# The opening of a fused attention and gated-unit kernel: another way to turn batch 0's q, more filler products, a split copy and an earlier sigmoid table

## Chip, cores and metric

One NeuronCore of one Trainium2 chip. The metric is the time of one execution in device microseconds. The engines are named as in the profile: PE is TensorE (its weight loads are PEld), DVE is VectorE, ACT is ScalarE, POOL is GpSimd, SP is the queue that issues most DMAs.

## What is computed

A linear attention without softmax for 8 batches, 8 heads, 576 tokens and a head size of 64, with a root-mean-square norm per head, followed by a gated linear unit whose gate comes from a causal convolution of 5 taps. All is fp32; the weights of the second block arrive as 64-bit floats.

```python
def _attn_ref(q, k, v, g_norm):
    kv = np.einsum('bhsd,bhse->bhde', k, v)
    out = np.einsum('bhsd,bhde->bhse', q, kv)
    rms = np.sqrt(np.mean(out * out, axis=-1, keepdims=True) + 1e-06)
    return (out / rms * g_norm).astype(np.float32)

# x: out with the heads side by side, (8, 576, 512)
def _moe_ref(x, w_val, conv_w, w_out):
    xp = np.concatenate([np.zeros((B, K - 1, D)), x], axis=1)
    for k in range(K):
        gate_pre += conv_w[k][None, None, :] * xp[:, k:k + S, :]
    gate = 1.0 / (1.0 + np.exp(-gate_pre))
    val = x @ w_val
    return (gate * val @ w_out).astype(np.float32)
```

## The kernel before

The order of all work is written out by hand. `PLAN` is one long string of 1,235 steps, such as `kv_product 0 1 @ 4 3`; the loop at the end of the kernel calls the function of that name with the numbers ahead of `@` as arguments, and the numbers behind it choose the buffers (for PSUM, one of eight banks) that the step writes. Steps are put on the engines' queues in exactly this order, and each engine works through its own queue in order; a later step of another engine can overtake only where it waits for nothing. Semaphores between engines follow from the buffers.

What each batch goes through:

- `load_q_rows` or `load_q`, `load_half`: q, k and v come in by DMA. For batches 0 and 1, q comes as rows (`load_q_rows`: 128 partitions, each one head and one of 32 tokens, 18 blocks of 64 values along the free axis, for the two halves r of the heads). Batch 0's v and one half of its q are issued from ACT's queue, the rest from SP's. SP's queue then holds the loads of `w_val` (`stage_weight`), and behind them q of batch 1.
- `turn_q_rows b j` (L511): turns four of the 18 blocks of q (two for j = 4) so that the head's 64 values lie along partitions. Each block and half is one fp32 product with the identity, 64 output partitions by 128, so 36 products for a batch. `sort_q b j` (L518): ACT copies the bank into `qT` with the tokens in the order of the convolution.
- `kv_product b i` (L474): k transposed times v, 72 products of 64 by 64 for each of two halves. `kv_copy b s` (L484 for batch 0, L487 for others): ACT copies the result to SBUF; for batch 0 into the block diagonal `kv_bd`, one copy for each of two row halves, so four in all.
- `raw_whole` (L546, batch 0), `raw_pair` and `raw_tail` (L535, other batches): q times kv. Then `square` (ACT), `sums` (DVE), `powers` (POOL), `normalise` (DVE for batch 0, ACT for the others).
- `turn_x`, `keep_x` (L617, L624) or `turn_blocks`, `move_blocks`: x is turned so that channels lie along partitions. `halo` (POOL) fills the columns that the convolution looks back to.
- `gate_start` (ACT, L649), `gate_tap` (DVE, L655), `gate_end` (ACT, L662, the sigmoid), `val_product` (L667) or `val_fast` (L716), `keep_val` (L676), `gated` (DVE, L680), and the last product `fast_product` (L807) and `out_product` (L754) with copies and `store`.

The weights come in as 64-bit floats and are narrowed to fp32 in eight small steps, `narrow_weight key part n`: n = 0, 5, 6, 4 and 7 on DVE (L397, L414, L419, L409, L423), n = 1, 2 and 3 on ACT (L402, L404, L406). `cw` (the convolution's taps, with the norm's weights in one more row) is narrowed first, `turn_cw` (L448) transposes it on PE and `keep_cw` (L452 to L454) scales it on DVE.

In the opening, `start_warm 36` (L464) puts 36 products of 32 by 32 columns of the identity on PE ahead of everything else; their result isn't used. `warm_up` (L329) applies the sigmoid to one column and stands late in the plan, at batch 7.

The steps of the opening as the plan has them:

```
load_q_rows 0 1; load_q_rows 0 0; load_half v 0 1; load_half k 0 1; start_warm 36; load_half v 0 0; load_half k 0 0;
stage_weight cw 0; turn_q_rows 0 1; turn_q_rows 0 3; turn_q_rows 0 0; kv_product 0 1; sort_q 0 1; stage_weight wval 1;
turn_q_rows 0 4; stage_weight wval 0; sort_q 0 3; stage_weight wval 3; sort_q 0 4; sort_q 0 0; kv_product 0 0;
narrow_weight cw 0 0; 0 5; 0 6; 0 1; 0 2; 0 3; turn_q_rows 0 2; narrow_weight wval 1 0; kv_copy 0 1;
narrow_weight wval 1 5; kv_copy 0 0; narrow_weight cw 0 4; wval 1 1; cw 0 7; load_q_rows 1 0; raw_whole 0 3;
narrow_weight wval 1 6; sort_q 0 2; load_q_rows 1 1; ...
```

Of the kernel before, what the change touches and what calls it, by code (L numbers as in the profile page):

```python
# [15 lines left out]
P = 128  # L16
# [3 lines left out]
load_q_rows 0 1; load_q_rows 0 0; load_half v 0 1 @ 0; load_half k 0 1 @ 0; start_warm 36 @ 0;  # L20
load_half v 0 0 @ 0; load_half k 0 0 @ 0; stage_weight cw 0 @ 0; turn_q_rows 0 1 @ 1; turn_q_rows 0 3 @ 0;
turn_q_rows 0 0 @ 2; kv_product 0 1 @ 4 3; sort_q 0 1 @ 0; stage_weight wval 1; turn_q_rows 0 4 @ 5;
stage_weight wval 0; sort_q 0 3; stage_weight wval 3; sort_q 0 4; sort_q 0 0; kv_product 0 0;
narrow_weight cw 0 0 @ 0; narrow_weight cw 0 5 @ 0; narrow_weight cw 0 6 @ 1; narrow_weight cw 0 1;
narrow_weight cw 0 2; narrow_weight cw 0 3; turn_q_rows 0 2 @ 2; narrow_weight wval 1 0 @ 1; kv_copy 0 1;
narrow_weight wval 1 5 @ 0; kv_copy 0 0; narrow_weight cw 0 4; narrow_weight wval 1 1; narrow_weight cw 0 7;
load_q_rows 1 0; raw_whole 0 3 @ 5; narrow_weight wval 1 6 @ 2; sort_q 0 2; load_q_rows 1 1;
narrow_weight wval 0 5 @ 1; narrow_weight wval 1 2; stage_weight wout 1 @ 0; narrow_weight wval 0 6 @ 0;
turn_cw @ 2; raw_whole 0 4 @ 4; load_half k 1 0; square 0 3 @ 0; narrow_weight wval 0 0 @ 0;
stage_weight wval 2; raw_whole 0 2 @ 3; narrow_weight wval 1 3; keep_cw; load_half v 1 0; sums 0 3 @ 0 0;  # L30
square 0 4 @ 1; load_half v 1 1; raw_whole 0 1 @ 2; narrow_weight wval 3 5 @ 1; load_half k 1 1;
narrow_weight wval 1 4; square 0 2 @ 0; powers 0 3; raw_whole 0 0 @ 0; stage_weight wout 0 @ 1;
narrow_weight wval 0 1; sums 0 4; load_q 2 2; sums 0 2; narrow_weight wval 0 2; narrow_weight wval 1 7;
square 0 0 @ 0; powers 0 2; narrow_weight wval 3 0 @ 1; square 0 1 @ 1; sums 0 0; turn_q_rows 1 0 @ 1;
narrow_weight wval 0 3; sums 0 1; turn_q_rows 1 4 @ 6; normalise 0 3 @ 0; turn_q_rows 1 2 @ 7; powers 0 1;
narrow_weight wout 1 5 @ 2; sort_q 1 4 @ 0; narrow_weight wval 3 1; narrow_weight wval 0 4; turn_x 0 3 @ 5;
normalise 0 2 @ 1; turn_q_rows 1 3 @ 6; keep_x 0 3; narrow_weight wval 0 7; narrow_weight wval 3 2;
turn_x 0 2 @ 3; narrow_weight wout 1 0 @ 0; normalise 0 4 @ 0; sort_q 1 0; narrow_weight wout 1 6 @ 0;
sort_q 1 2; turn_x 0 4 @ 5; load_half v 2 1 @ 0; turn_q_rows 1 1 @ 1; narrow_weight wval 3 3;
normalise 0 0 @ 1; normalise 0 1 @ 0; keep_x 0 2; turn_x 0 0 @ 0; keep_x 0 4; narrow_weight wval 3 6 @ 2;  # L40
narrow_weight wout 1 1; turn_x 0 1 @ 2; load_half k 2 0 @ 0; halo 0; narrow_weight wval 3 4; keep_x 0 0;
kv_product 1 0 @ 5 3; narrow_weight wval 2 5 @ 1; keep_x 0 1; narrow_weight wval 3 7; gate_start 0 0 @ 0;
narrow_weight wval 2 0 @ 1; val_product 0 0 1 @ 2; narrow_weight wval 2 6 @ 2; stage_weight wout 3 @ 2;
gate_start 0 1 @ 1; gate_tap 0 0 3; narrow_weight wval 2 1; gate_tap 0 1 3; narrow_weight wval 2 2;
val_product 0 0 0 @ 0; load_half v 2 0 @ 0; gate_tap 0 0 2; narrow_weight wval 2 3; gate_tap 0 0 1; sort_q 1 3;
gate_start 0 3 @ 2; gate_tap 0 1 2; kv_product 1 1; load_half k 2 1 @ 0; keep_val 0 0 0;
narrow_weight wval 2 4; narrow_weight wout 1 2; val_product 0 1 0 @ 0; gate_tap 0 0 0; narrow_weight wout 1 3;
narrow_weight wval 2 7; kv_copy 1 1; kv_copy 1 0; gate_end 0 0; gate_tap 0 3 3; keep_val 0 0 1;
raw_tail 1 @ 5 3; narrow_weight wout 0 0 @ 1; raw_pair 1 3 @ 7 6; gate_tap 0 3 2; square 1 4 @ 1;
narrow_weight wout 0 1; gated 0 0; val_product 0 1 1 @ 2; square 1 3 @ 0; sums 1 4 @ 0 0; gate_tap 0 3 1;  # L50
gate_start 0 2 @ 0; powers 1 4; keep_val 0 1 0; sums 1 3; sort_q 1 1; val_product 0 2 0 @ 4; gate_tap 0 3 0;
square 1 2 @ 1; powers 1 3; narrow_weight wout 0 2; gate_tap 0 2 3; narrow_weight wout 0 3;
narrow_weight wout 1 4; val_product 0 3 1 @ 1; normalise 1 4 @ 0; turn_q 2 2 @ 1; gate_tap 0 1 1;
keep_val 0 1 1; normalise 1 3 @ 1; load_q 3 1; sums 1 2; turn_x 1 4 @ 2; raw_pair 1 1 @ 5 3; gate_tap 0 2 2;
powers 1 2; keep_val 0 2 0; narrow_weight wout 1 7; gate_end 0 3; val_product 0 3 0 @ 0; load_q 2 0;
narrow_weight wout 0 4; square 1 0 @ 1; narrow_weight wout 0 5 @ 0; keep_x 1 4; square 1 1 @ 0;
narrow_weight wout 3 0 @ 0; sums 1 0; load_q 2 1; normalise 1 2 @ 0; turn_x 1 3 @ 2; sums 1 1;
val_product 0 2 1 @ 4; powers 1 0; gate_tap 0 2 1; keep_val 0 3 0; narrow_weight wout 3 5 @ 2;
# [171 lines left out]
def kernel(  # L230
# [11 lines left out]
    nc = tc.nc  # L242
    B, H, S, D = q.shape
# [640 lines left out]
```

## Time and profile before

| what | value |
|---|---|
| median of 3 runs | 304.96 us (304.31 to 306.63) |
| the profiled execution's own time | 305.64 us |
| its span (first to last instruction) | 303.9 us |
| mean granted TensorE clock in it | 0.991 |
| DVE busy, ACT busy, POOL busy | 88%, 64%, 39% of the span |
| largest L474 rows (kv_product) | 1,008 records, 17.3 us busy |
| ACT_TABLE_LOAD | two, 1.28 us each, at 2.23 and 38.07 us |

All times inside the execution are counted from the span's start. In a timeline row the columns are: start, duration, engine, line, operation, output and inputs with their sizes, the number of records, and in brackets the idle time of the engine just before and what ended it. An fp32 product appears as two records, each with a weight load of its own; a transpose appears as one. In a row of stages the columns are the stage, its length, the busy time of the engine with its records, the granted clock (1.00 is full speed), the DMA engines' busy share and GB/s. In the chain of waits each piece is start, duration, engine, tile and line; "issue" is time in which the engine waited for nothing that the profile shows. A queue's row gives its packets, megabytes and share of 16 DMA engines' time.

### The profile page before, as it was taken

To read this page: it belongs to the slowest core of one execution; us is meant where nothing else is said; L and a number is where in the kernel's file an instruction comes from. 1 tells how busy PE (TensorE), PEld (TensorE's weight loads), DVE (VectorE), ACT (ScalarE), POOL (GpSimd) and SP (SyncE) were. 2 spreads that over 40 slices of the span, in tenths; PEclk is the share of its full clock that TensorE was granted. 3 is DMA by queue.
4 is the path that set the end of the run, shared out by engine and by line. 5 is a ranking of instruction groups with operands and counts; after the bars stand their busy time and mean duration, and the time that the engine had idled before them with its cause. 6 is when DMAs were issued, how large, how long until landed. Compare 5 with 4: busy or idle time off the path is not lost.

```text
span 303.9 us, 8964 instructions
## 1 busy us (share of the span) xinstructions
PE 290.4 (96%) x3441; PEld 231.4 (76%) x3441; DVE 266.9 (88%) x474; ACT 194.5 (64%) x596; POOL 117.1 (39%) x127
## 2 busy tenths in 40 slices
PE   6698999999999999999999989999999999999993
PEld 6586877888888588878877567788877588888582
DVE  1189999999999999999999989999989999999512
ACT  1488999999658836767678437585567665525120
POOL 3037146418455417604775357142473174000000
PEclk9979999999999999999999999999999999999998
DMA  7979966669658688786679776864521144222423
GB/s 272 371 254 382 292 245 194 187 208 286 177 144 267 201 241 241 201 244 175 155 225 281 203 188 169 251 202 108 141 61 45 35 119 108 55 52 52 106 69 104
DMA packets 32075, 55.53 MB, mean 183 GB/s; under 512 B 6167, under 2 KB 14359, under 8 KB 32033
## 3 DMA queue, kind: packets, MB, share of 16 engines
q1 hardware_dynamic: 29520, 49.76, 56.2%
q0 software_dynamic: 1632, 3.17, 4.4%
q10 hardware_dynamic: 880, 2.03, 1.8%
q8 instruction: 27, 0.44, 0.6%
q14 instruction: 16, 0.12, 0.1%
HBM read 39.21 MB, written 9.44 MB: 160 GB/s over the span
## 4 chain that ended last, share of the span: by engine, by line
PE 83%; ACT 7%; DMA 4%; DVE 3%; issue 1%; ACTq 0%
PE bank L807 33%; PE bank L716 27%; PE bank L667 5%; PE bank L474 5%; PE bank L535 5%; PE bank L754 5%; DMA v<-in_v_dram 4%; ACT x L605 1%; PE bank L617 1%; PE bank L511 1%; ACT gate L649 1%; DVE ss L578 1%; ACT sq L569 1%; ACT wexp L406 1%; ACT wexp L404 1%
## 5 line engine op out<-in xcount | busy, mean ns | idle before, releaser
L586 POOL TENSOR_TENSOR rt<-ss,mhalf 128x8 f32<-128x8 f32 (+3 forms) x38 | 70.5, 1864 | 91.5 <-DVE ss L578 91.3
L655 DVE SCALAR_TENSOR_TENSOR gate<-xT,cwT,gate 128x576 f32<-128x576 f32 x128 | 101.0, 804 | 0.4
L605 ACT ACTIVATE x<-bank,rt 128x64 f32<-128x64 f32 x252 | 56.1, 379 | 7.1 <-POOL rt L586 6.8
L807 PE MATMUL bank<-wsum,w 128*128 128x256 f32 x192 | 48.5, 382 | 0.0
L638 POOL DMA_DIRECT2D xT<-y x48 | 26.6, 560 | 37.6 <-DVE y L630 13.5
L807 PEld LDWEIGHTS bank<-wsum,w 128*128 128x128 f32 x192 | 35.7, 190 | 6.7 <-issue 1.2
L716 PE MATMUL bank<-xs,vsum 128*128 128x288 f32 x144 | 38.1, 407 | 0.0
L667 PE MATMUL bank<-xT,wval 128*128 128x288 f32 x128 | 33.5, 411 | 0.0
L716 PEld LDWEIGHTS bank<-xs,vsum 128*128 128x128 f32 x144 | 27.2, 190 | 7.1
L807 PE MATMUL bank<-wout,gv 128*128 128x256 f32 x128 | 32.4, 381 | 0.0
L662 ACT ACTIVATE gate<-gate 128x576 f32<-128x576 f32 x32 | 22.6, 710 | 10.8 <-DVE gate L655 10.7
L817 DVE TENSOR_TENSOR ot<-bank,ot 128x256 f32<-128x256 f32 (+1 forms) x32 | 17.2, 547 | 13.0 <-PE bank L807 10.3
L667 PEld LDWEIGHTS bank<-xT,wval 128*128 128x128 f32 x128 | 23.6, 190 | 6.1
L569 ACT ACTIVATE sq<-bank 128x256 f32<-128x256 f32 (+1 forms) x70 | 21.8, 376 | 10.0 <-PE bank L535 9.6
L716 PE MATMUL bank<-xT,wval 128*128 128x288 f32 x96 | 27.0, 410 | 0.0
L807 PEld LDWEIGHTS bank<-wout,gv 128*128 128x128 f32 x128 | 24.1, 190 | 3.6
L649 ACT ACTIVATE gate<-xT,cwT 128x576 f32<-128x576 f32 x32 | 24.8, 787 | 1.9 <-DVE gv L680 1.6
L578 DVE TENSOR_REDUCE ss<-sq 128x8 f32<-128x520 f32 (+1 forms) x40 | 24.6, 625 | 0.9 <-ACT sq L569 0.7
L680 DVE TENSOR_TENSOR gv<-gv,gate 128x576 f32<-128x576 f32 x32 | 23.8, 748 | 0.2
L474 PE MATMUL bank<-v,k 64*64 64x64 f32 x1008 | 17.3, 220 | 4.7 <-DMA v<-in_v_dram 2.7
L535 PEld LDWEIGHTS bank<-kv,qT 64*64 64x64 f32 x1008 | 16.7, 134 | 6.5 <-issue 3.6
L474 PEld LDWEIGHTS bank<-v,k 64*64 64x64 f32 x1008 | 15.9, 135 | 7.5 <-issue 3.6
(90 smaller groups left out, 458.4 us busy)
## 6 DMA issues: line engine op xcount, KB each, us to landing
qs<-in_q_dram SPq DMA_DIRECT2D x96, 140.0 KB, 3.8
out_dram<-ot SPq DMA_DIRECT2D x140, 64.0 KB, 1.7
k<-in_k_dram SPq DMA_DIRECT2D x14, 576.0 KB, 5.9
v<-in_v_dram SPq DMA_DIRECT2D x12, 576.0 KB, 5.1
xT<-y SPq DMA_DIRECT2D x48, 64.0 KB, 2.6
xT<-y POOLq DMA_DIRECT2D x48, 64.0 KB, 2.7
y<-in_moe_w_val_dram SPq DMA_DIRECT2D x4, 512.0 KB, 12.1
w<-in_moe_w_out_dram SPq DMA_DIRECT2D x4, 512.0 KB, 9.7
```

The source lines that it names most:

```text
L474: nc.tensor.matmul(st["kvps", b][s][r * D:(r + 1) * D, i], st["k", b, i][rows, r, cols], st["v", b, i][rows, r, cols], start=(j == 0), sto ...
L535: nc.tensor.matmul(st["raw", b, c][r][cols, to * D:(to + 1) * D], st["qT", b][rows, hp, first:first + D], kvs[b % 2][rows, hp, :], start=T ...
L569: nc.scalar.activation(out=sq[:, r * n // 2:(r + 1) * n // 2, 0:D], in_=raw.rearrange("p (h e) -> p h e", e=D), func=AF.Square)
L578: nc.vector.reduce_sum(out=st["ss", b][:, FIRST[c]:FIRST[c] + n], in_=st["sq", b, c][:, 0:n], axis=AX.X)
L586: nc.gpsimd.tensor_tensor(out=st["rt", b][:, which], in0=st["ss", b][:, which], in1=mhalf[:, which], op=ALU.pow)
L605: nc.scalar.activation(out=x[:, to * D:(to + 1) * D], in_=raw[:, h * D:(h + 1) * D], func=AF.Copy, scale=root[:, to:to + 1])
L638: (nc.sync if i % 2 else nc.gpsimd).dma_start(out=xTs[b % 2][i * TB:(i + 1) * TB, :, first:first + P], in_=y[a * TB:(a + 1) * TB, i])
L649: nc.scalar.activation(out=gate[:], in_=xTs[b % 2][:, jt, HALO:SX], func=AF.Copy, scale=cwT[:, K - 1, jt:jt + 1])
L655: nc.vector.scalar_tensor_tensor(out=gate[:], in0=xTs[b % 2][:, jt, tap * TB:tap * TB + S], scalar=cwT[:, tap, jt:jt + 1], in1=gate[:], op ...
L667: nc.tensor.matmul(val[:], wval[:, kc, jt * P:(jt + 1) * P], xTs[b % 2][:, kc, HALO + n * SV:HALO + (n + 1) * SV], start=(kc == 0), stop=( ...
L716: nc.tensor.matmul(st[bank, "val", b, mj][:], weights_[:, k], tokens()[:, k], start=(n in (0, 1, 3) and k == 0), stop=(k == NK // 2 - 1), ...
L807: nc.tensor.matmul(st[bank, i, p], tokens()[:, k], weights_[:, k], start=(n < 2 and k == 0), stop=(k == NK // 2 - 1), skip_group_check=True)
```

## The change

Batch 0's q is turned by transposes: two neighbouring blocks of a half together make a 128 by 128 square, and one transpose turns both, so 18 transposes take the place of 36 products. The two blocks then lie in the bank's two partition halves, and `sort_q` for batch 0 takes four copies in place of one: the even blocks by ACT, the odd ones by DVE. Batch 1 is turned as before.

`start_warm` is called four times, with a width: 43 products of 32 columns at the start, 9 of 64 columns ahead of the first kv_product, 24 behind it and 7 behind the second, all in a bank of their own. For batch 0, `kv_copy` gives the second row half to DVE. `warm_up` moves from batch 7 to the opening, ahead of the first copy on ACT. In the plan all five `turn_q_rows 0` now stand ahead of the first kv_product, all five `sort_q 0` right behind it, the narrowing of `cw` is finished ahead of the second kv_product, and the narrowing of `wval` starts behind the kv copies. No other step is moved.

```diff
-start_warm 36 @ 0
+start_warm 43 32 @ 7
 load_half v 0 0 @ 0; load_half k 0 0 @ 0; stage_weight cw 0 @ 0
+warm_up
 turn_q_rows 0 1 @ 1; turn_q_rows 0 3 @ 0; turn_q_rows 0 0 @ 2
+turn_q_rows 0 4 @ 5; turn_q_rows 0 2 @ 6; start_warm 9 64 @ 7
 kv_product 0 1 @ 4 3
+start_warm 24 64 @ 7
 sort_q 0 1 @ 0
+sort_q 0 3; sort_q 0 0; sort_q 0 4; sort_q 0 2
 stage_weight wval 1
-turn_q_rows 0 4 @ 5
 stage_weight wval 0
-sort_q 0 3
 stage_weight wval 3
-sort_q 0 4; sort_q 0 0; kv_product 0 0
 narrow_weight cw 0 0 @ 0; narrow_weight cw 0 5 @ 0; narrow_weight cw 0 6 @ 1
 narrow_weight cw 0 1; narrow_weight cw 0 2; narrow_weight cw 0 3
-turn_q_rows 0 2 @ 2
+narrow_weight cw 0 4; narrow_weight cw 0 7; kv_product 0 0; start_warm 7 64 @ 7; kv_copy 0 1; kv_copy 0 0
 narrow_weight wval 1 0 @ 1
-kv_copy 0 1
 narrow_weight wval 1 5 @ 0
-kv_copy 0 0; narrow_weight cw 0 4
 narrow_weight wval 1 1
-narrow_weight cw 0 7
 load_q_rows 1 0; raw_whole 0 3 @ 5; narrow_weight wval 1 6 @ 2
-sort_q 0 2
...
-warm_up
```

```diff
+    PAIRED_Q = (0,)
...
-    def start_warm(n):
+    def start_warm(n, width):
+        bank = ps([TB, P], f"warm{n}")
         for _ in range(n):
-            nc.tensor.matmul(warm_bank()[0:TB, 0, 0:TB], ident[:, 0:TB], ident[:, 0:TB], start=True, stop=True)
+            nc.tensor.matmul(bank[0:TB, 0:width], ident[:, 0:TB], ident[:, 0:width], start=True, stop=True)
...
-                nc.scalar.copy(
+                (nc.vector.tensor_copy if r else nc.scalar.copy)(
                     out=kv_bd[rows, :, rows].rearrange("p (i s) e -> p s i e", s=2)[:, s], in_=ps_[rows])
...
     def turn_q_rows(b, j):
-        pq = ps([P, HB, P], f"qTps{b}_{j}")
+        st["pq", b, j] = pq = ps([P, HB, P], f"qTps{b}_{j}")
+        if b in PAIRED_Q:
+            for r in range(2):
+                for n in range(0, m, 2):
+                    nc.tensor.transpose(
+                        pq[:, r * 2 + n // 2, :],
+                        qs[:, r, j * HB + n:j * HB + n + 2, :].rearrange("p n d -> p (n d)"), ident[:])
+            return
...
     def sort_q(b, j):
+        qT, pq = new_qT(b)[:].rearrange("p h (n t) -> p n h t", t=TB), st["pq", b, j][:].rearrange(
+            "p n (h t) -> p n h t", t=TB)
+        if b not in PAIRED_Q:
+            nc.scalar.copy(out=qT[:, j * HB:j * HB + m], in_=pq[:, 0:m])
+            return
+        for r in range(2):
+            for e in range(2):
+                (nc.vector.tensor_copy if b == 0 and e else nc.scalar.copy)(
+                    out=qT[r * D:(r + 1) * D, j * HB + e:j * HB + m:2],
+                    in_=pq[e * D:(e + 1) * D, r * 2:r * 2 + m // 2])
```

## The prediction

> **What bounds the kernel now.** I read the page's busy times and chain first, then the timeline of the opening engine by engine, then the granted clock by stage, and last the chain late in the span.
>
> ```profile
> PE 290.4 (96%) x3441; PEld 231.4 (76%) x3441; DVE 266.9 (88%) x474; ACT 194.5 (64%) x596; POOL 117.1 (39%) x127
> PE 83%; ACT 7%; DMA 4%; DVE 3%; issue 1%; ACTq 0%
> q8 instruction: 27, 0.44, 0.6%
> ```
>
> TensorE carries 83% of the chain. From 52.46 us (first piece: L617, released by ACT) the chain stays on it to the last product, so whatever TensorE gains or loses by then, or in a gap later, reaches the end.
>
> ```profile
> 9.47 1.28 PE L474 MATMUL bank<-v,k 64*64 64x64 f32 x72 [0.33 <-DMA v<-in_v_dram]
> 13.72 1.29 PE L474 MATMUL bank<-v,k 64*64 64x64 f32 x72 [2.39 <-DMA v<-in_v_dram]
> 14.94 1.97 PE L511 MATMUL bank<-ident,qs 128*64 128x128 f32 x16
> 16.84 1.83 PE L546 MATMUL bank<-kvbd,qT 128*128 128x128 f32 x8
> 14.99 0.43 DVE L397 TENSOR_SCALAR wexp<-y 128x512 uint32<-128x512 uint32 x1 [6.04 <-DMA y<-in_moe_w_val_dram]
> 18.87 0.16 DVE L452 TENSOR_SCALAR gcol<-bank 128x1 f32<-128x1 f32 x1 [0.61 <-PE bank L448]
> ```
>
> TensorE waits for v, then crawls: 16 records of L511 in 1.97 us, against 16 in 1.09 at 25.63. The clock rows say why:
>
> ```profile
> 11.40:14.80 3.40, 1.08 (x72) 1.00 1.09 353
> 14.80:18.30 3.50, 3.50 (x39) 0.51 0.51 139
> 25.10:28.50 3.40, 2.65 (x28) 1.00 1.06 389
> ```
>
> After a stretch only 1.08 of 3.40 us busy the grant is 0.51 for one stretch. But VectorE, once wval lands at 14.99, has a single real gap (0.61 at 18.87) and is busy 2.96 of 3 us, 4.00 of 4 and 5.00 of 5 up to 50 us. It sets the opening's pace, not TensorE.
>
> ```profile
> 172.14 2.07 PE bank L474 x139
> 174.20 1.81 issue
> 176.01 0.34 PE bank L474 x5
> ...
> 206.19 2.02 PE bank L474 x126
> 208.21 0.21 issue
> 208.42 0.50 PE bank L474 x17
> ```
>
> The two gaps late in the chain, 2.02 us, lie inside the kv_products of batches 6 and 7, and no engine or data transfer ends them.
>
> **The change part by part** (against the profiled run: span 303.90, its time 305.64, 1.74 outside the span; the median, 304.96, is 0.68 lower, and I carry differences over to it).
>
> *Opening fillers.* 36 products took 1.36 to 5.14 us, 0.107 each. Seven more end at 5.6 to 5.9, under the wait for q (L511 starts at 6.09): nothing; uncovered, at most 0.75.
>
> *Transposes.* Gone: 36 products of L511, 3.05 + 0.66 + 1.97 = 5.68 us of TensorE. New: 18 transposes; L617's eight in 1.09 us give 0.136 each, 2.45 in all, done at 8.6. Nine 64-wide fillers follow. Such a record is worth half of L546's 128-column one (32 in 3.54: 0.11), so 0.11 a product and 1.0 us to 9.6, where v and k now let the first kv_product start at 9.47: +0.1, with no one waiting. The 24 more (2.6 us) run 10.9 to 13.5, inside the old 2.39 gap, before v at 13.68: nothing; the clock should stay up.
>
> *Sorting q.* Five ACT copies become ten on ACT and ten on DVE, and in the built order they alternate: each DVE copy waits for ACT's, and ACT's second for DVE's. ACT 128x256 is 0.37 (L518), DVE's nearest is L830, 128x256, 0.42. Half the partitions may not change that; bounds 0.30/0.33 and 0.45/0.60 (L817's queued 0.55). Per chunk 0.37 + 0.42 + 0.42 and three hand-overs near 0.025: 1.28. Four chunks and a half-size one (0.9) from 6.78 end at 12.8 to 13.1. Queued behind them on DVE is cw's narrowing: 0.2 us, then three ACT steps (12.12 to 13.39: 1.27), then 0.55 on DVE: done at 15.1 instead of 16.26, in time for the kv copies. Slack is some 0.3 us; 15 serial steps, each 0.03 slower, use it up, and beyond that VectorE pays one for one: the worst prices cost 1.3.
>
> *kv copies.* The product still ends at 15.01. ACT's two take 0.53 (four took 1.07 from 15.06). DVE's two, 0.28 each (L830 less 128 elements), end at 16.0. raw_whole starts at 16.05 instead of 16.84, at full clock: turn_cw's result comes by 17.4, not 18.85. The seven fillers (0.8) fit before.
>
> *VectorE's queue, which decides.* wval's narrowing now starts behind the kv copies, at 16.05, not 14.99 (+1.06); the two cw steps that lay within it (15.67 to 16.19) have gone ahead (-0.52), and so has the 0.61 gap. Net -0.1: the throttle's 1.7 us and the earlier products buy almost nothing, since VectorE is late next.
>
> *Sigmoid's table.* One load (the 1.28 at 2.23) moves to the first sigmoid and serves all; the second, 1.28 at 38.07, goes. ACT is on the chain there, but gate_end's last tap ends on VectorE at 38.36, where ACT started at 39.37: 1.0 at most. At 41.70 ACT reuses the gate room that VectorE's L680 frees at 41.49: 0.2 there, with VectorE's 0.1, 0.3. With that TensorE starts at 52.16. The late warm_up (0.22 on ACT, 64% busy): nothing.
>
> *SP and POOL.* q of batch 1 no longer waits for L511's end (16.92). The DMA share is 0.04 to 0.09 between 16 and 17.5, so those transfers move up; nothing on the chain waits for them.
>
> *Instruction blocks.* 27 packets on q8 for 2 x 3,441 TensorE records is one per 255. Up to the gap at 174.20 the trace counts 2,502 pairs, up to the one at 208.21 2,879: 754 records, with 14 waits in the program between them 768 = 3 x 256. So both gaps stand at block borders. A q8 packet falls in 173.0 to 174.6 and in 205.7 to 207.2, just ahead of each restart. In both products the border before lies under 25 instructions from the start, so one whole block is small products, 1.9 us (144 records take 2.10 at 143.43), while asking for a block and having it took 172.1 to 176.0, 3.9. The change adds 47 fillers of 4 instructions, drops 36 products of 4, adds 18 transposes of 2 and drops two waits: +78. Every border falls 78 instructions earlier in the work. Batch 6's product then has one border 202 instructions in, the one before it back in L754's slow products; batch 7's is 176 in. Both gaps should go: -2.0. In batch 5 a border comes to stand at the raw_tail just ahead, the next 225 into the product, 1.9 us later. The fetch starts early there, since slow products come before, as at 205.7 (gap 0.21); I take +0.5 between 0 and 1.8.
>
> The Trainium skill, Runtime: NRT & Kernel Launch, Instruction fetch mechanics, has the same blocks of 256, but gives TensorE's buffer 2,048 instructions and calls a border mostly hidden. By that rule the term is nil and the sum -0.3; the gaps 768 instructions apart speak against it.
>
> Sum: -0.3 - 2.0 + 0.5 = -1.8: 303.84 profiled, 303.2 by the median.
>
> **The rivals.** One per cent, 3.05 us, is about what a measurement of this kernel can tell from no change.
>
> *Borders cost nothing or the gaps stay* (the fetch may have been late for another reason: only two gaps): the opening's 0.3 alone, 304.7. For it: other borders fell in kv_products without a gap. Against: none of those had a whole block inside one.
>
> *The opening gives back.* If transposes don't count as work for the clock, the stretch 4.6 to 8.0 is one third busy and the grant is halved from 8.0 to 11.4. Then 3.4 us do 1.7 us of work, the fillers ahead of the second kv_product end near 15.1, not 13.5, and VectorE waits 1.3 more. Or the copies cost their worst, also 1.3. Either way 304.5. Against the first: from 25.1 to 28.5 ten transposes make 1.7 of the 2.65 busy us and the grant stays 1.00, while 1.08 busy us lost it. The Trainium skill, TensorE: Matmul & The Clock Gate, PE-mode transpose, says that they don't count as busy the same way; that row disagrees.
>
> *Slower: new gaps replace the old.* The borders come to stand 36 into batch 1's first product and 115 into its second, some 5.9 us apart (the products start at 30.45 and 35.7). The border near there now was crossed at 31.3 and answered by a packet only in 36.5 to 38.2, with all DMA engines busy; with 1.3 to the restart that is 8.0, a gap of 2.1 at 36.4. ACT has 0.6 us of slack there (kv at 37.65, its product done at 37.06), so 1.5 is paid; batch 5 pays 1.8. -0.3 - 2.0 + 1.5 + 1.8 = +1.0: 306.0. It decides once new gaps together pass 2.3 us. Against: DMA work moves up into the hole at 16, and the earlier borders were answered in 2 to 3 us.
>
> *More.* With their slow restarts the two products took 4.22 and 2.73 against 2.10: 2.75. No new gap: -3.05, 301.9.
>
> **Numbers.** Forecast 0.50; borders free 0.18; opening gives back 0.12; slower 0.10; more 0.10. The likeliest is 303.2. Leaving out one in ten at each side, the range runs from the best case, 301.9, to between opening and new gaps, 305.6. Faster by over 1% (under 301.9): half of "more" and the forecast's edge where fetches also cost least, 0.15; slower by over 1% (over 308.0) needs new gaps and worst copies together, 0.05; within, 0.80.
>
> **What would show it.** Right: clock 1.00 from 4.6 on; sort copies alternating and done by 13.1; raw_whole at 16; gcol within 0.3 us of 18.8; one table load; TensorE's gaps near 172 and 206 gone, any new one at 143.4 or 36.4. Wrong: gcol before 18.2 (VectorE was not the bound) or after 19.5 (copies or clock); gaps of the old size at the old places (the border count fails).

## The result, and the profile after

The changed kernel takes 307.43 us (median of 18 runs, 306.04 to 309.37), the kernel before, run beside it, 304.95 (18 runs, 304.08 to 307.23). The ratio is 1.0074 with a 95% interval of 1.0053 to 1.0095: slower by some 2.3 us, within one per cent, where I had forecast 303.2. The profiled execution has a span of 306.2 us and a time of 308.0, against 303.9 and 305.64.

The page of the changed kernel, its busy times, the shares of its chain by engine and by line, and its queue of instruction blocks:

```profile
PE 293.3 (96%) x3481; PEld 233.2 (76%) x3481; DVE 273.0 (89%) x486; ACT 193.7 (63%) x598; POOL 114.6 (37%) x127
PE 70%; DVE 12%; SPq 6%; DMA 5%; ACT 3%; issue 2%; POOL 1%; DVEq 0%; ACTq 0%
PE bank L817 23%; PE bank L726 21%; PE bank L677 11%; PE bank L471 5%; PE bank L545 4%; PE bank L764 4%; SPq L648 3%; SPq L849 3%; DMA xT<-y 2%; DVE gate L665 2%; DVE xs L711 2%; DMA qs<-in_q_dram 2%; PE bank L627 1%; DVE qT L528 1%; DVE ss L588 1%
q8 instruction: 27, 0.44, 0.6%
```

TensorE's share of the chain fell from 83% to 70%, and what came in has names that were not there before: SP's queue (L648 is `move_blocks`, L849 `store`), the transfers xT<-y that `move_blocks` issues, and `x_sums` (L711) on DVE, which waits for them. `move_blocks` carries x, turned in blocks by DVE, over to the rows of xT; TensorE's `val_fast` needs it and `x_sums`.

The opening went nearly as forecast. TensorE's timeline (L471 is kv_product, L461 the fillers, L556 raw_whole):

```profile
9.53 1.28 PE L471 MATMUL bank<-v,k 64*64 64x64 f32 x72
10.74 3.05 PE L461 MATMUL bank<-ident 128*32 128x64 f32 x48
13.86 1.28 PE L471 MATMUL bank<-v,k 64*64 64x64 f32 x72
16.16 1.16 PE L556 MATMUL bank<-kvbd,qT 128*128 128x128 f32 x8
20.06 2.16 PE L556 MATMUL bank<-kvbd,qT 128*128 128x128 f32 x17 [1.22 <-issue]
```

VectorE's (L528 the copies of q, L398 the first step on wval, L453 the norm's weights):

```profile
12.97 0.43 DVE L528 COPY qT<-bank 64x256 f32<-64x256 f32 x1 [0.43 <-ACT qT L528]
16.14 0.43 DVE L398 TENSOR_SCALAR wexp<-y 128x512 uint32<-128x512 uint32 x1
19.07 0.16 DVE L453 TENSOR_SCALAR gcol<-bank 128x1 f32<-128x1 f32 x1
```

And the clock, in the rows by stage:

```profile
11.40:14.80 3.40, 3.33 (x103) 3.01 (x104) 1.78 (x7) 2.04 (x6) 0.00 (x0) 1.00 1.10 355
14.80:18.30 3.50, 3.37 (x57) 2.82 (x50) 3.15 (x9) 2.23 (x6) 0.00 (x0) 1.00 1.07 392
```

The crawl at 0.51 is gone, raw_whole starts 0.68 us sooner than before, yet gcol comes 0.20 later, as VectorE's queue sets it. A gap of 1.22 us inside raw_whole, ahead of 20.06, is new: a block's border lies there too, which the prediction doesn't name. It cost nothing that shows: at 28 us TensorE is 0.16 us later than before, and 0.26 in after_0 (below), which has no gap there. The difference of the end arises behind the opening. In the chain of waits (start, duration, piece; "issue": nothing in the profile ended it), batch 1's second kv_product now has a gap, and those of batches 6 and 7 have none:

```profile
35.97 1.01 PE bank L471 x57
36.98 1.27 issue
38.25 0.46 PE bank L471 x15
...
145.71 2.16 PE bank L471 x144
147.86 0.56 SPq L648
148.43 0.04 issue
148.47 1.06 SPq L648
...
155.09 3.10 DMA xT<-y
...
158.50 0.77 DVE xs L711
...
175.35 2.33 PE bank L471 x144
...
208.01 2.26 PE bank L471 x144
```

At 253 us of the kernel before's time TensorE has a new wait, which the profile puts down to these transfers; in its timeline:

```profile
255.75 2.18 PE L726 MATMUL bank<-xT,wval 128*128 128x288 f32 x8 [0.91 <-DMA xT<-y]
```

To see where the time goes I take the same TensorE record in two profiles and subtract its starts, each counted from its span's start: TensorE's lateness, in us, against the kernel before. The columns are places in the kernel before's time: behind batch 1's kv_product (38), 52, and so on, up to the last product. The other rows are runs that the next section explains.

| run | 38 | 52 | 90 | 140 | 158 | 172 | 177 | 182 | 209 | 252 | end |
|---|---|---|---|---|---|---|---|---|---|---|---|
| changed kernel | 1.70 | 1.41 | 1.56 | 2.27 | 3.18 | 3.42 | 1.33 | 1.82 | 1.34 | 1.16 | 2.23 |
| before_78 | 1.84 | 1.55 | 2.99 | 2.99 | 4.28 | 4.29 | 2.18 | 3.13 | 2.65 | 2.47 | 3.27 |
| after_0 | 0.25 | 0.05 | 0.04 | 0.47 | 0.97 | 0.97 | 0.86 | 0.86 | 0.51 | 0.33 | 0.40 |
| before_late80 | | 0.00 | 0.82 | 1.96 | 2.50 | 2.69 | 0.60 | 1.32 | 0.84 | 0.65 | 1.33 |
| after_lateloads | 0.47 | 0.29 | 1.08 | 1.20 | 2.06 | 3.05 | 0.96 | 1.27 | 1.28 | 1.28 | 1.78 |
| after_m34b | 0.18 | 0.01 | 0.01 | 0.01 | -0.05 | -0.05 | -2.16 | -1.53 | -0.81 | -0.58 | -0.29 |
| after_placed | 0.60 | 0.42 | 0.42 | | 0.21 | 0.52 | -1.58 | -1.43 | -1.91 | -1.95 | -1.44 |

The first row is the ledger of the change: 0.16 from the opening, 1.54 in batch 1's gap, 0.29 back by 52, then 0.15, 0.71, 0.91 and 0.24 lost between 52 and 172, 2.09 regained where batch 6's gap was, 0.49 lost again, 0.48 regained in batch 7 and 0.18 behind it, and 1.07 lost at 253. The old gaps are paid back in full, 2.6 us, and more than that is lost elsewhere. It is the ledger of one profile: executions differ, as the next section says.

### The profile page after: what moved, and what is told of

Read it like the earlier page. It is cut to its first block, busy times and chain, and to the rows that moved or that the text cites. A ratio compares the mean times of both kernels' runs of the same rounds, so it can differ in the third digit from the quotient of the medians.

```text
span 306.2 us, 9057 instructions
## 1 busy us (share of the span) xinstructions
PE 293.3 (96%) x3481; PEld 233.2 (76%) x3481; DVE 273.0 (89%) x486; ACT 193.7 (63%) x598; POOL 114.6 (37%) x127
## 4 chain that ended last, share of the span: by engine, by line
PE 70%; DVE 12%; SPq 6%; DMA 5%; ACT 3%; issue 2%; POOL 1%; DVEq 0%; ACTq 0%
PE bank L817 23%; PE bank L726 21%; PE bank L677 11%; PE bank L471 5%; PE bank L545 4%; PE bank L764 4%; SPq L648 3%; SPq L849 3%; DMA xT<-y 2%; DVE gate L665 2%; DVE xs L711 2%; DMA qs<-in_q_dram 2%; PE bank L627 1%; DVE qT L528 1%; DVE ss L588 1%
## 5 line engine op out<-in xcount | busy, mean ns | idle before, releaser
L648 POOL DMA_DIRECT2D xT<-y x48 | 26.7, 560 | 38.5 <-DVE y L640 8.3
L677 PEld LDWEIGHTS bank<-xT,wval 128*128 128x128 f32 x128 | 23.6, 190 | 6.1
L817 PEld LDWEIGHTS bank<-wout,gv 128*128 128x128 f32 x128 | 24.1, 190 | 3.6
L726 PEld LDWEIGHTS bank<-xT,wval 128*128 128x128 f32 x96 | 17.6, 190 | 6.4 <-DVE gate L665 1.3
L545 PE MATMUL bank<-kv,qT 64*64 64x64 f32 x1008 | 19.1, 221 | 0.2 <-ACT x L615 0.2
```

The costliest lines, as they stand in the source:

```text
L545: nc.tensor.matmul(st["raw", b, c][r][cols, to * D:(to + 1) * D], st["qT", b][rows, hp, first:first + D], kvs[b % 2][rows, hp, :], start=T ...
L648: (nc.sync if i % 2 else nc.gpsimd).dma_start(out=xTs[b % 2][i * TB:(i + 1) * TB, :, first:first + P], in_=y[a * TB:(a + 1) * TB, i])
L677: nc.tensor.matmul(val[:], wval[:, kc, jt * P:(jt + 1) * P], xTs[b % 2][:, kc, HALO + n * SV:HALO + (n + 1) * SV], start=(kc == 0), stop=( ...
L726: nc.tensor.matmul(st[bank, "val", b, mj][:], weights_[:, k], tokens()[:, k], start=(n in (0, 1, 3) and k == 0), stop=(k == NK // 2 - 1), ...
L817: nc.tensor.matmul(st[bank, i, p], tokens()[:, k], weights_[:, k], start=(n < 2 and k == 0), stop=(k == NK // 2 - 1), skip_group_check=True)
```

## The experiments

Each was run beside the kernel before on the same chip, whose median lay between 305.59 and 306.45; a ratio (with its 95% interval) is to the kernel before that ran beside it. A profile is one execution: kernels that are alike up to 150 us differ there by up to 2 us among themselves, so the ratios carry the verdicts on totals, and the profiles those on places. All profiles agree on where the borders are. In 22 places of the 20 profiles TensorE starts its next record over 0.5 us after the last one, released by nothing in the trace, and 1.2 to 1.6 us after the end of a block's packet; in all 22 the number of its records ahead, weight loads and waits included, is 193 modulo 256.

**What part of the change costs it: the count of TensorE's instructions, or the rest?** Two kernels on each side. An fp32 product counts 4 instructions, a transpose 2. `start_warm n width turns` adds `turns` small transposes; fillers wider than 128 columns read kv_bd; no result of a filler is used.

before_clock (the fillers keep the clock, the count stays):

```diff
-start_warm 36 @ 0
+start_warm 31 32 2 @ 0
 ...
 turn_q_rows 0 4 @ 5
+start_warm 4 192 @ 7
```

> The kernel before, with TensorE kept busy in its wait for v (31 fillers of 32 columns and two transposes first, then four fillers of 192 columns between the two kv_products), so that the clock should stay near 1.00 from 4.6 to 18 us; TensorE's instruction count is the old one to within one, so every block border stays where it was. Borders theory (the time is set by where the borders of 256 instructions fall): the two gaps of batches 6 and 7 stay, the restored clock changes the end by under 0.3 us: 304.6 to 305.2. Rival (the crawl at half clock did cost): 1.0 to 1.7 us faster, 303.3 to 304.0.

before_78 (the change's 78 instructions alone):

```diff
 turn_q_rows 0 4 @ 5
+start_warm 19 32 1 @ 7
```

> The kernel before with 19 fillers of 32 columns and one transpose added between the two kv_products of batch 0: 78 more TensorE instructions, so every later border falls where it does in the changed kernel; q, the copies and the table load are as before. Borders theory: a gap of 1.2 to 1.5 us in batch 1's second kv_product near 36.5, no gap in batches 6 and 7, and new waits on xT<-y later on: 306.5 to 308. Rival (the later waits come from the rest of the new opening, above all batch 1's q loaded 7 us earlier): only the gaps move, -2.6 + 1.4, so 303.6 to 304.0.

after_0 (the change without them):

```diff
-start_warm 24 64 @ 7
+start_warm 4 256 1 @ 7
```

> The changed kernel with four fillers of 256 columns and one transpose in place of the 24 fillers of 64 columns: about the same busy time, 78 TensorE instructions fewer, so every later border falls where it did before the change. Borders theory: batch 1's gap of 1.27 us goes, the gaps in batches 6 and 7 (1.8 and 0.2 us) are back, the later waits on xT<-y shrink: 304.6 to 305.4. Rival (the rest of the new opening): the later waits stay and the old gaps are added, -1.4 + 2.6 on 307.4: 308 to 309.

after_m34:

```diff
-start_warm 43 32 @ 7
+start_warm 35 64 @ 7
 ...
-start_warm 24 64 @ 7
+start_warm 4 256 @ 7
```

> The changed kernel with 35 fillers of 64 columns in place of 43 of 32, and four of 256 in place of 24 of 64: 112 TensorE instructions fewer than in the changed kernel, 34 fewer than before the change. Borders then stand some 8 us apart around batch 1's products, 4.5 us apart in batch 6's, and in batch 7's a whole block lies inside the products but its fetch starts early, in slow products. Borders theory: no gap in batches 1 and 6, at most 0.5 us in batch 7: 302.6 to 304. Rival (the rest of the new opening makes the later waits): 306 to 306.6.

| run | ratio | interval |
|---|---|---|
| before_clock | 0.9997 | 0.9959 to 1.0034 |
| before_78 | 1.0074 | 1.0035 to 1.0112 |
| after_0 | 0.9985 | 0.995 to 1.002 |
| after_m34 | 1.0026 | 0.9986 to 1.0066 |

The count alone makes the kernel before as slow as the changed one; without the count, the changed kernel is no slower than before. The clock alone, and the transposes, the split copies, the table and batch 1's earlier q together, matter by no more than the intervals. TensorE's timeline of before_78 has the changed kernel's gap, at the same 57th record:

```profile
35.94 1.08 PE L473 MATMUL bank<-gv 64*64 64x64 f32 x57
38.40 0.46 PE L473 MATMUL bank<-gv 64*64 64x64 f32 x15 [1.38 <-issue]
```

and that of after_0 has none there, but the old one in batch 6 again, at the 139th record as before:

```profile
35.99 1.28 PE L474 MATMUL bank<-gv 64*64 64x64 f32 x72
...
172.92 2.26 PE L474 MATMUL bank<-v,k 64*64 64x64 f32 x139
176.87 0.34 PE L474 MATMUL bank<-v,k 64*64 64x64 f32 x5 [1.69 <-issue]
```

after_m34 was to be faster, 302.6 to 304, but its wider fillers pushed the transposes back by 0.9 us, so it says little; after_m34b below mends that.

**Is it batch 1's gap?** Theory 1 says so: the gap is paid, and what it delays makes later transfers late. Theory 2: the later borders.

before_late80 puts the 80 instructions behind batch 1, by doing five products of `val_product` as two column halves (the halves alternate within one PSUM bank, and these five products lose part of their sums; before_late80c does one half after the other):

```diff
+HALVED = ((0, 2, 0), (0, 3, 1), (0, 3, 0), (0, 2, 1), (0, 1, 1))
 ...
-            nc.tensor.matmul(val[:], wval[...], xTs[...][...], ...)
+            for part in range(2 if (b, jt, n) in HALVED else 1):
+                nc.tensor.matmul(val[:, cols], wval[...], xTs[...][...][:, cols], ...)
```

> The kernel before, with five val_products of batch 0 (run between 40 and 50 us) made of two column halves each: the same work in 20 more products, 80 more TensorE instructions, which move every border from 50 us on to within two instructions of the changed kernel's, while batch 1's products keep the old borders. Theory 1 (batch 1's gap makes the change slower): no gap anywhere, so faster than before: the late gaps' 2.6 us less what the split costs (at most 1.0) and less what the next wait takes back; -0.5 to -2.0, ratio 0.993 to 0.998. Theory 2 (the later borders' places, in batches 2 to 7, make the later waits): slower than before, ratio 1.002 to 1.005, with the same late waits on xT<-y.

before_stall delays TensorE and moves no border behind:

```diff
-start_warm 36 @ 0
+start_warm 34 32 @ 0
 ...
+start_warm 2 256 @ 7
 kv_product 1 1
```

> The kernel before with two fillers of 256 columns put ahead of batch 1's second kv_product (some 1.46 us of TensorE) and two fillers fewer in the opening, so that every border behind that place is where it was. A pure delay of TensorE where the changed kernel has its gap. Theory 1a (a delay there is paid, and makes later transfers late too): ratio 1.005 to 1.009, with new waits on xT<-y later on. Theory 1b (paid and no more): +1.2 to 1.5, ratio 1.004 to 1.005. Theory 2 (delays there are absorbed; something else slows the changed kernel): ratio under 1.002.

after_m34b:

```diff
-start_warm 43 32 @ 7
+start_warm 35 32 @ 7
 ...
-start_warm 24 64 @ 7
+start_warm 4 256 @ 7
```

> The changed kernel with 35 fillers of 32 columns in place of 43, and four of 256 columns in place of 24 of 64: 112 TensorE instructions fewer. The run with 35 fillers of 64 columns began its transposes 0.9 us late; this one should not. No gap in batches 1 and 6, none or little in batch 7. Theory 1 with the late gaps paid in full: 2.6 less than before, ratio 0.992. Theory 1 with the late gaps taken back by the next wait on xT<-y: within 0.5 us of before, ratio 0.998 to 1.001. Theory 2 (not batch 1's gap): ratio above 1.003.

after_lateloads (`hold`: ACT writes one column of the room that the first of these loads fills):

```diff
-load_half v 2 1 @ 0; ... load_half k 2 0 @ 0; ... stage_weight wout 3 @ 2; ... load_half v 2 0 @ 0; ... load_half k 2 1 @ 0
 kv_copy 1 0
+hold; load_half v 2 1 @ 0; load_half k 2 0 @ 0; stage_weight wout 3 @ 2; load_half v 2 0 @ 0; load_half k 2 1 @ 0
```

> The changed kernel with five loads for batch 2 and wout (2.8 MB, issued from 26.8 to 33.7 us) held back until ScalarE has copied batch 1's kv (some 38 us), so that the transfers should run dry near 33 us and the instruction block asked for at 31.0 should come in 1 to 3 us instead of 4.8. No TensorE instruction is added or moved. Theory 1 (batch 1's block is late because data transfers fill the engines): its gap of 1.27 shrinks below 0.3 and the time goes to that of before or under, ratio 0.996 to 1.001. Rival (a block takes that long there anyway): gap and ratio stay, 1.007.

| run | ratio | interval |
|---|---|---|
| before_late80 | 1.0041 | 1.001 to 1.0073 |
| before_stall | 1.0027 | 0.9993 to 1.0062 |
| after_m34b | 0.9986 | 0.9957 to 1.0016 |
| after_lateloads | 1.0075 | 1.0041 to 1.011 |

Theory 1 falls as the main cause. With batch 1 untouched and no gap in any product, before_late80 is still slower, by 0.4% or 1.3 us, and its row in the table loses at the same places, 88, 126 to 140, 155 and 253. The stall's fillers ran 1.05 us; by its ratio it is 0.8 us slower, and the interval holds both nothing and 1.9, so a plain delay at that place isn't priced. after_lateloads settles why batch 1's block is late. In the changed kernel TensorE crosses the border ahead of it at 30.89 and the block starts to come at 35.67, with the transfer engines full; with the loads held back it starts at 31.51, 0.30 us after the border, and the product runs through:

```profile
36.21 1.28 PE L463 MATMUL bank<-gv 64*64 64x64 f32 x72
```

Still the total did not move: TensorE lost at 88, 155 and 172 what it had gained at 38. (Loads that come later may cost something of their own there; the run can't part that.) after_m34b has no gap in batches 1 and 6 and gained 2.1 us at 177, and by 209 three fifths of it were gone again. Its ratio, 0.9986, is what theory 1 had forecast and below the 1.003 of theory 2; but it moves every border behind the opening as well as batch 1's, so it can't part the two as I had meant it to.

**What takes the time at those places?** The transfers' landing marks give it. Each DMA lands in 16 pieces. In the changed kernel the last xT<-y of batch 4, issued at 155.09, has fifteen pieces in 2.1 us later and the sixteenth at 158.19, 1.0 after them; a block for TensorE is under way from 155.91 to 156.84. SP's issue at 148.47 in the chain above, 1.06 us instead of 0.60, coincides with the block from 148.12 to 149.14. Over all 20 profiles of this study, behind 45 us (of the transfers, those whose 16 marks are all in the trace):

| | block under way | none |
|---|---|---|
| xT<-y transfers | 776 | 907 |
| of them, last piece over 0.5 us behind the fifteenth | 475 | 90 |
| median us from issue to landing | 3.38 | 2.38 |
| SP's DMA issues | 553 | 5,467 |
| of them over 0.95 us long | 257 | 1 |
| median and longest us of one issue | 0.80, 2.22 | 0.42, 0.96 |

So theory 3: a block, one packet of 16 KB and 0.9 to 1.9 us long (median 1.1), holds up SP's next issues and one piece of the transfers under way. Where these are the last xT<-y of a batch, `x_sums` and TensorE wait. The Trainium skill, DMA: Bandwidth & Descriptors, section "Issuing engines are not separate DMA queues", says that transfers run on the same 16 engines and interleave whoever issues them; the late sixteenth piece agrees, if a block rides on one of them, which the trace doesn't name.

A first try to use it: two kernels with other borders throughout, chosen by this theory from the kernel before's profile, and the late shift with 24 more.

before_late80c:

```diff
+        for half in range(halves):
+            for kc in range(NK):
+                nc.tensor.matmul(val[:, cols], wval[...], xTs[...][...][:, cols], ...)
```

> The kernel before with five val_products of batch 0 done as two column halves one after the other (80 more TensorE instructions between 40 and 50 us), computing the same: borders behind 50 us as in the changed kernel to within two instructions, batch 1's as before. Theory 3 (the instruction block of 16 KB comes in over one of the 16 transfer engines and holds up the pieces of other transfers there for about 1 us; with these borders it hits the last xT<-y transfers of batches 2, 4 and 7, and x_sums and TensorE wait): block transfers near 156 and 249 us, the last xT<-y transfers near 157 landing 1.0 to 1.8 us behind their other fifteen pieces, ratio 1.003 to 1.005. Theory 1 (batch 1's gap alone slows the changed kernel): ratio under 1.000.

before_late104 (`(0, 1, 0)` is halved too):

```diff
-start_warm 36 @ 0
+start_warm 38 @ 0
```

> As the kernel with 80 more instructions late, but with six val_products halved and two more fillers in the opening: 104 more, so every border behind 50 us falls 24 instructions earlier still, some 2.5 us earlier where the products are large. Theory 3: the block near 156 us is now in by 152 and the one near 249 by 246, ahead of the last xT<-y transfers; these land together with their other pieces, TensorE loses under 0.3 us at 155 and 254 instead of 0.75 and 0.7, and the ratio falls to 0.997 to 1.001. Rival (any such shift, or the halves themselves, cost it): ratio as with 80, 1.003 to 1.005.

before_m56:

```diff
-start_warm 36 @ 0
+start_warm 22 64 @ 0
```

> The kernel before with 22 fillers of 64 columns in place of 36 of 32, nothing else: 56 TensorE instructions fewer, so every border falls 56 later. By the borders of the kernel before I work out: none of 256 instructions run off in under 2.3 us but in batch 7's products, where the block is fetched early; no block falls on the last xT<-y transfers of batches 3, 4 and 7. Theory 3: 0.4 to 1.5 us faster, ratio 0.995 to 0.999. Rival (borders matter only through gaps inside products, each paid in full): 2.0 faster, 0.9935. Rival (borders do not matter): 1.000.

after_m54:

```diff
-start_warm 43 32 @ 7
+start_warm 30 32 @ 7
 ...
-start_warm 24 64 @ 7
+start_warm 4 256 @ 7
```

> The changed kernel with 30 fillers of 32 columns in place of 43 and four of 256 in place of 24 of 64: 132 TensorE instructions fewer, borders within two of those of the kernel before with 56 fewer. What the rest of the change is worth on the same borders: theory 3 as before: the ratio of the run with 56 fewer less 0.000 to 0.002: 0.993 to 0.998. Rival (the new opening costs something by itself): 1.001 or more.

| run | ratio | interval |
|---|---|---|
| before_late80c | 1.004 | 1.0008 to 1.0073 |
| before_late104 | 1.0121 | 1.0089 to 1.0152 |
| before_m56 | 1.0119 | 1.0072 to 1.0166 |
| after_m54 | 1.0117 | 1.0088 to 1.0146 |

before_late80c repeats the 0.4%. The other three came out the wrong way: slower than any kernel yet. I had looked for cheap places behind 45 us alone. Ahead of that the transfer engines are full, and blocks start 1.1 to 7.2 us after the border in these three. In before_m56 one border fell into batch 0's second kv_product; TensorE's timeline:

```profile
12.43 1.02 PE L473 MATMUL bank<-v,k 64*64 64x64 f32 x50 [1.19 <-DMA v<-in_v_dram]
15.77 0.91 PE L473 MATMUL bank<-v,k 64*64 64x64 f32 x22 [2.32 <-issue]
```

after_m54 has one of 1.25 there too, and another new gap of 1.20 at 36.8. before_late104 lost 1.1 in a new gap at 57.8, and by that delay the block that I had placed at 151 met batch 4's transfers after all, at 155.21; another, from 127.68 to 128.89, met batch 3's last xT<-y, whose sixteenth piece landed 1.4 behind the rest, and TensorE waited 0.97 at 131.6 for a step of VectorE that stands behind x_sums. The mechanism is in these profiles, but as a forecast of totals the theory had failed, and a test was due in which only one block moves.

**One block moved past, onto and ahead of one group of transfers.** Nothing changes before 216 us. Products of `fast_product` and `val_fast` are halved behind that, two, seven or fourteen of them, so that the block which comes at 255.2 in the kernel before comes earlier. Batch 7's xT<-y go out from 244.4 to 251.6.

```diff
+HALVED = (("fast_product", 1, 2, 2), ("fast_product", 1, 3, 2), ...)
 ...
+        halves = 2 if ("fast_product", i, p, n) in HALVED else 1
+        for half in range(halves):
             for k in range(NK // 2):
-                nc.tensor.matmul(st[bank, i, p], tokens()[:, k], weights_[:, k], ...)
+                nc.tensor.matmul(st[bank, i, p][:, cols], tokens()[:, k], weights_[:, k][:, cols], ...)
```

> The kernel before with two products of the last stretch (217 to 219 us) done as two column halves each: 16 more TensorE instructions from there on, nothing else. The block that came at 255.2 should come near 253.5 to 254, when batch 7's last xT<-y transfers (issued 244.4 to 251.6, landed by 253.5) are over. Theory 3 (a block's transfer holds up SyncE's DMA issues and one piece of each transfer under way): TensorE loses at most 0.2 us from 240 to 256, ratio 0.998 to 1.002. Rival (any shift costs, or the halves do): some 0.1 us.

> As the run with 16 more instructions, but seven products halved from 217 us on: 56 more. The block should come near 249 to 250, amid SyncE's six issues of xT<-y for batch 7 (247.7 to 251.6). Theory 3: one of these issues takes 1 to 1.7 us in place of 0.6, the last transfer lands 0.5 to 1.2 us later, x_sums and TensorE with it: +0.5 to +1.1 us between 240 and 256, kept to the end, ratio 1.0015 to 1.004. Rival (the block matters only by gaps in small products): no loss, ratio 0.999 to 1.001.

> As before, but fourteen products halved from 217 us on: 112 more. The block should come near 243, while SyncE has no xT<-y to issue (241.7 to 244.4). Theory 3: at most 0.2 us lost between 240 and 256, ratio 0.998 to 1.0015, although twice as many products are halved as in the run with 56. Rival (the halves cost it, or the shift as such): twice the loss of the run with 56, +1 to +2 us.

A fourth kernel, placed, puts the borders of batches 5 to 7 where the theory calls them cheap: nine products halved from 159 to 168 us (`val_fast 4 0 2` to `fast_product 1 1 5`) and five from 217 us on.

> The kernel before with nine products halved from 159 to 168 us (72 more instructions: batch 6's and 7's kv_products no longer hold a whole block) and five more from 217 us on (40 more: the block near 255 comes ahead of batch 7's xT<-y transfers, near 243). Up to 158 us all is as before. Theory 3: the gaps of 1.8 and 0.2 us and their slow restarts go (-2.1 and -0.5), 0.5 to 0.9 comes back as the block near 177 meets batch 5's xT<-y transfers, nothing at 254: 1.2 to 2.1 us faster, ratio 0.993 to 0.996. Rival (VectorE sets the pace anyway and takes back all of it): 0.999 to 1.001.

| run | ratio | interval | block, us | TensorE's lateness at 240, 256 |
|---|---|---|---|---|
| end16 | 0.9994 | 0.9964 to 1.0025 | 254.73 to 256.08 | 0.19, 0.17 |
| end56 | 1.0045 | 1.0016 to 1.0073 | 250.70 to 252.16 | 1.18, 2.16 |
| end112 | 1.0028 | 0.9994 to 1.0061 | 245.44 to 246.45 | 0.75, 1.05 |
| placed | 1.0006 | 0.9981 to 1.0031 | 246.00 to 246.87 | 0.88, 0.91 |

SP's timeline, the six issues of xT<-y (start, sum of the six from first to last end), of end16:

```profile
247.74 3.87 SPq L640 DMA_DIRECT2D xT<-y  x6
```

of end56:

```profile
248.80 5.04 SPq L641 DMA_DIRECT2D xT<-y  x6
```

and of end112:

```profile
248.87 3.86 SPq L643 DMA_DIRECT2D xT<-y  x6
```

TensorE's timeline of end56 shows who waits:

```profile
253.84 1.03 PE L816 MATMUL bank<-wout,gv 128*128 128x256 f32 x4
255.67 2.18 PE L722 MATMUL bank<-xT,wval 128*128 128x288 f32 x8 [0.80 <-DMA xT<-y]
```

The loss of 0.98 comes with the block on the transfers and goes when it is on either side (-0.02, 0.30), though end112 has twice the halves of end56; there the block caught one earlier issue (1.2 us long). The landing marks agree: in end56 eight of the last twelve transfers have their sixteenth piece 0.8 to 1.8 us behind the fifteenth, in end16 none of batch 7's over 0.3, in end112 none over 0.7. What TensorE had lost before 216 us, 0.3 to 0.8, is the scatter of like executions. That is the causal test of theory 3, at one place and in one profile of each. In the totals end56 alone is clear of no change, the three intervals overlap, and end112's 1.0028 lies above the 1.0015 that I had allowed it. The halves themselves cost nothing that shows; in placed, sixteen records of half width take 2.12 us, where eight whole ones of the same line took 2.10 before:

```profile
165.87 2.12 PE L724 MATMUL bank<-xs,vsum 128*128 128x144 f32 x16
```

placed gained 1.57 us behind 158 in its profile, within what was expected, but by then this profile was 2.48 late, though the kernel up to there is the kernel before (its granted clock is 0.5 from 24.1 to 27.5). Its ratio shows no gain: it lies where the rival had it. So the same placing went onto the changed kernel with its borders put back:

```diff
-start_warm 24 64 @ 7
+start_warm 4 256 1 @ 7
 ...
+HALVED = (("val_fast", 4, 0, 2), ("val_fast", 4, 1, 2), ..., ("fast_product", 1, 1, 5),
+          ("fast_product", 1, 2, 2), ("fast_product", 1, 3, 2), ("fast_product", 1, 2, 4),
+          ("fast_product", 1, 2, 5), ("fast_product", 1, 2, 6))
```

The five of the last two lines are left out in after_mid.

> The changed kernel with the fillers of the run with its borders put back (four of 256 columns and one transpose for the 24), nine products halved from 159 to 168 us and five from 217 us on, as in placed. Theory 3: no gap in batches 1, 6 and 7 and no block on batch 7's last xT<-y transfers: 1.2 to 2.1 us less than the run with the borders put back alone (0.9985), ratio 0.991 to 0.995. Rival (the next wait takes all of it back): 0.998 to 1.000.

> As after_placed without the five late halves: the block that follows 231 us should come near 249 to 251, on batch 7's xT<-y transfers. Theory 3: 0.5 to 1 us more than after_placed, lost by TensorE between 246 and 256 us; ratio 0.993 to 0.998. Rival: the same as after_placed.

after_placed: 0.9946, 0.9912 to 0.9981; the medians alone, 305.58 us against 306.45, would give 0.997. after_mid: 0.998, 0.994 to 1.002; its block came from 247.32 to 248.56, one of its xT<-y issues took 1.5 us, and TensorE's lateness went from -0.20 to 0.53 between 246 and 256, where after_placed lost 0.51 with its block from 242.77 to 243.88 on the first of these issues. The two ratios differ as expected, by 1.0 us, but their intervals overlap, and the losses at this place differ by 0.2 us only. The chain of after_placed by engine:

```profile
PE 91%; DVE 6%; ACT 1%; issue 1%; POOL 0%; POOLq 0%
```

With the borders placed so, TensorE has 91% of the chain, and the kernel is faster than the kernel before and the changed one. What the placing adds to after_0 the totals don't show: after_0's interval (0.995 to 1.002) and this one overlap.

## Why the prediction was wrong, and where it was right

- **Fillers, transposes, clock.** Right. The first fillers end at 5.82; the 18 transposes took 2.19 us for my 2.45; the clock is 1.00 from 5.2 us on, and its mean 0.996 or more in all 18 runs. The crawl that this removes is not in every execution of the old opening: end16 and end112 ran without it. The 24 fillers took 3.05 for 2.6, and the second kv_product began 0.14 later, as its v landed at 13.81 in place of 13.68.
- **Sorting q.** The alternation is as told; the last copy ends at 13.40 for 12.8 to 13.1, cw is done at 15.58 for 15.1. The slack covered nearly all of it: raw_whole began 0.11 later than forecast.
- **kv copies and VectorE's queue.** Right: raw_whole at 16.16 (16.05), wval from 16.14 (16.05), gcol at 19.07, 0.27 above the 18.8 of the sum.
- **Sigmoid's table.** One load, as told, and 0.29 us regained by 52. But before_78 and before_stall, with both loads, regain 0.29 there too: the size came out, the reason isn't shown.
- **SP and POOL.** q of batch 1 went out 8 us sooner (8.95, not 16.94) and nobody on the chain gained or lost by it, as after_0 shows. On equal borders all these parts together are worth -0.46 us (0.9985), with an interval of -1.5 to +0.6 around it; the sum had -0.3.
- **Instruction blocks: the step that failed.** The forecast was -2.0 for the old gaps and +0.5 for new ones; the term for new losses is the one that was too small. The positions were right: the gaps of batches 6 and 7 went, and batch 5 had none, since its block came early (144.33, before the product). Two things were not. First, the sum left out batch 1, where the text has a border 115 into the second product; I had it under the slower rival, at one in ten, arguing that earlier borders were answered in 2 to 3 us. The block took 4.78 to start, and TensorE lost 1.54. Second, and larger, the premise of the first part: "the chain stays on it to the last product, so whatever TensorE gains or loses by then, or in a gap later, reaches the end". A border was priced only by TensorE's own gap. The runs showed that a block also costs whoever is issuing or transferring, and that a gap regained is partly waited away: -2.6 became -2.1 in batches 6 and 7 net of 0.49, and the same shift lost 3.1 us at 88, 126 to 158, 172 and 253 in this profile. That blocks do this is tested by moving one of them at 253 alone; for the other places it is read from the landing marks, and the sizes stay open. The kernel before's chain, on TensorE from 52.46 us on, didn't show these transfers; their landing marks were there to be read.
- **The rule on blocks.** The Trainium skill, Runtime: NRT & Kernel Launch, section "Instruction fetch mechanics", calls the crossing of a block's border mostly hidden. By that rule before_78 would have been even with the kernel before; it measured 1.0074. The runs disagree.
- **The rivals.** The slower one named batch 1's gap, and one in batch 5 that didn't come; its 306.0 was nearest to the result but by another sum, so that is luck. "The opening gives back" didn't come about: 2.19 us of transposes ran from 6.08, the clock stayed at 1.00, and the copies' extra time was hidden but for 0.1 us.

Not settled: why the losses at 88 and 126 vary so between runs with the same borders (0.15 in the changed kernel and 1.44 in before_78 at 88), and what a delay in batch 1 alone is worth.

## What to carry to other kernels

When a change adds or drops TensorE instructions, count them modulo 256 and test the count alone, with fillers of another width or products done in halves, before anything else is concluded from one or two microseconds. Where TensorE waits on transfers or comes close to it, its gaps are not the whole price of a block's border: look at which DMA issues and landings each block meets. A share of 83% in the chain of waits says who ended last, not that time saved there is kept.

## What the runs showed of the hardware

- Behind 45 us a block starts to come 0.9 us after TensorE has crossed the border ahead of it (median of 440; four in five lie between 1.8 us ahead of the crossing and 2.1 behind). Before 45 us, where the transfer engines are nearly full, the median of 100 is 2.8 and the longest 7.2. In all 22 gaps at a border of over 0.5 us (from one record's start to the next's), TensorE went on 1.24 to 1.56 us after the packet's end.
- While a block is under way, SP's DMA issue of 0.42 to 0.60 us stretches to as much as 2.22; outside of that, one of 5,467 passed 0.95. POOL's issues of the same transfers do not stretch (0.55 median and at most 0.64 in both cases).
- A product of 288 columns done as two of 144 takes TensorE no longer, and so moves the borders at no price.
